# A linear-attention and SwiGLU block on one core: Q and K weights loaded together in 2 KB rows, token tiles loaded in pairs, and a new order of phase 1

## The chip, the cores and the metric

The kernel runs on one core of a Trainium2 chip. The metric is the device time of one execution in microseconds (us). A profiled execution gives the trace. In the profile PE is TensorE's matmuls and PEld its weight loads, DVE is VectorE, ACT is ScalarE, POOL is GpSimd, SP is SyncE, which here only issues DMAs.

## What is computed

```python
x = A_x                                   # [1, 2048, 512], bf16
xn = layernorm(x)                         # over the 512 columns, eps 1e-5
q, k, v = split(xn @ wqkv)                # wqkv [512, 1536]; 32 heads of 16
phi = lambda t: where(t > 0, t + 1, exp(t)) + 1e-6
kv = phi(k)^T v, z = sum over tokens of phi(k)        # per head
o = (phi(q) kv) / (phi(q) . z + 1e-6)
A = o @ wo                                # wo [512, 512]
B = (silu(xn @ w_gate) * (xn @ w_up)) @ w_down        # 512 -> 1792 -> 512
out = x + A + B
```

## The kernel before

The 2048 tokens are 16 tiles of 128, one token a partition. **Phase 1** handles each tile: load it, find mean and variance (`S`: `bn_stats`, line 260, and `bn_aggr`, line 266, on VectorE), 1/std on ScalarE (`R`, lines 275 and 277), normalise (`L` on VectorE, line 332; `P` on GpSimd, lines 347 and 350), transpose to columns x tokens, project to Q and K (`Q`, `K`: four matmuls of 512 columns each, one for each chunk of 128 rows of the weights, line 428), apply phi (exponential `y`, `x` on ScalarE, lines 446 and 449; clamp `n`, `m` on GpSimd, line 456; sum `u`, `s` on VectorE, line 467), and add the tile's part of G = xn^T phi(k) (`G`, four matmuls, line 477). V is never formed: kv comes from G and the V weights later (line 592). **Phase 2** computes gate and up (line 534), the product with silu, then for each tile the attention output and the down projection in one PSUM bank (lines 664 and 668), adds x (line 674) and stores.

Most tiles are transposed by DMA (`D`, line 406, SyncE's queue). The first four go another way. Tiles 0, 1 and 2 are only centred, not scaled; 1/std goes into the exponential's scale. They are *turned*: TensorE multiplies the raw x tile with an identity (`turn_x`, line 381) and adds minus the mean with a second product with a diagonal matrix of the mean (`turn_mean`, line 389; the diagonal at line 375, on VectorE by `a` or on GpSimd by `O`), and ScalarE or VectorE copy the halves out (`e`, `h` on ScalarE, line 398; `g`, `f` on VectorE, line 400). Tile 3 is normalised and then transposed on TensorE (`X`, line 362), and copied out by ScalarE (`Y`, line 370). The scaled copies that G needs of tiles 0 to 2 are `J` (GpSimd, line 327) and `j` (VectorE, line 319); `r` makes their powers of std on ScalarE.

The order is written out by hand. `load` (line 185) issues DMAs in two lists, one on SyncE's queue and one on ScalarE's, at the start: `h` is half a tile of x, `x` a tile, `Qc` and `Kc` chunk c of the Q or K weights. Then one long text names the steps; each step is added to its engine's list in the order of the text, and an engine works through its list in that order. `Q0:23` means chunks 2 and 3 of the Q projection of tile 0; `l` loads a tile on SyncE's queue; `F` is matmuls of 256 columns on constants, which keep TensorE busy (line 250, also used for warming up); `T0` to `T7` load the big weights on SyncE's queue (first halves of gate and up, V, wo, second halves of gate and up, two halves of down); `U` is the gate and up work of phase 2 brought forward. Waits between engines are found by `_Program` from the tiles that steps read and write.

Of the kernel before, what the change touches and what calls it, by code (L numbers as in the profile page):

```python
# [17 lines left out]
NDC = D // P  # L18
# [92 lines left out]


def bass_parallel_sum__linear_attn_block__swiglu_ffn__prompt_kernel(nc, A_x, A_wqkv, A_wo, B_x, B_w_gate, B_w_up, B_w_down, out):
    xin = A_x[0]
    oview = out[0]
    K = _Program()
    bf, f32 = dt.bfloat16, dt.float32

    with contextlib.ExitStack() as es:
        E = es.enter_context  # L120

        def sb(name, shape, dtype):
# [12 lines left out]
        wqkv = sb("wqkv", [P, NDC, 3 * D], bf)  # L135
# [18 lines left out]
        out_sb = sb("out_sb", [P, 2, D], bf)  # L154
# [25 lines left out]
        def B(i):  # L180
            return ("bank", i)


        def load(eng, key, dst, src):
            K.add(eng, lambda e: e.dma_start(dst, src), w=[key], dma=True)

        def xload(eng, t):
            load(eng, ("x", t), x_sb[:, t, :], xin[t * P:(t + 1) * P, :])

        def wload(eng, i, h=0, n=1):  # L190
            cs = slice(h * NDC // n, (h + 1) * NDC // n)
# [20 lines left out]
        H = D // 2  # L212

        def xhalf(eng, t, h):
            load(eng, ("x", t, h), x_sb[:, t, h * H:(h + 1) * H], xin[t * P:(t + 1) * P, h * H:(h + 1) * H])

        def wchunk(eng, i, c):
            load(eng, ("wqk", i, c), wqkv[:, c, i * D:(i + 1) * D], A_wqkv[c * P:(c + 1) * P, i * D:(i + 1) * D])

        for eng, text in (("sp", "h00 K0 x1 x3 Q1 K2"),  # L220
                          ("act", "h01 x2 Q0 Q3 Q2 K3 K1")):
            for w in text.split():
                if w[0] == "h":
                    xhalf(eng, int(w[1:-1]), int(w[-1]))
                elif w[0] == "x":
                    xload(eng, int(w[1:]))
                else:
                    wchunk(eng, int(w[0] == "K"), int(w[1:]))

        for i, v in enumerate((1e-5, math.log1p(1e-6), math.log(1e-6))):  # L230
# [3 lines left out]
            out=ident[:, :], in_=ident[:, :], compare_op=ALU.not_equal, fill=1.0,  # L234
# [159 lines left out]
        def turn_out(t, h, eng):  # L394
            src = banks[TURN_BANK[t] + h][:, 0:H].rearrange("p (c s) -> p c s", c=NDC // 2)
            dst = xcT[:, h * NDC // 2:(h + 1) * NDC // 2, t * P:(t + 1) * P]
            if eng == "act":
                K.add("act", lambda e: e.activation(dst, src, ACT.Copy), r=[B(TURN_BANK[t] + h)], w=[("xcT", t, h)])
            else:
                K.add("dve", lambda e: e.tensor_copy(dst, src), r=[B(TURN_BANK[t] + h)], w=[("xcT", t, h)])  # L400

# [16 lines left out]
        def proj(i, t, cs):  # L418
            if (i, t) not in at:
                at[i, t] = LOWBANK[i, t] if (i, t) in LOWBANK else nextbank()  # L420
                begun[i, t] = 0
            b, col = at[i, t], i * D
            src = xcT if t in CENTRED else xnT
            fns = []
            for c in cs:
                first, last = begun[i, t] == 0, begun[i, t] == NDC - 1
                begun[i, t] += 1
                fns.append(lambda e, c=c, first=first, last=last: e.matmul(  # L428
                    banks[b][:, :], src[:, c, t * P:(t + 1) * P], wqkv[:, c, col:col + D], start=first, stop=last))
            keys = sorted({("xcT", t, c // 2) for c in cs}) if t in CENTRED else xkeys(t)  # L430
            K.add("pe", fns, r=keys + [("wqk", i, c) for c in cs], w=[B(b)])
# [8 lines left out]
        def phi_exp(i, t):  # L440
            b = at[i, t]
            buf, bkey = ef[:, efslot(b), :], ("ef", efslot(b))
            if i == 0 and t in later:
                buf, bkey = pq[:, t, :], ("pq", t)
            if t in CENTRED:
                K.add("act", lambda e: e.activation(buf, banks[b][:, :], ACT.Exp, bias=lstd[:, t:t + 1], scale=rstd[:, t:t + 1]),  # L446
                      r=[B(b), ("rs", t), ("lstd", t)], w=[bkey])
            else:
                K.add("act", lambda e: e.activation(buf, banks[b][:, :], ACT.Exp), r=[B(b)], w=[bkey])  # L449

        def phi_min(i, t):
# [51 lines left out]
        def stat(t):  # L503
# [7 lines left out]
            "S": stat, "R": rs, "L": lna_dve, "P": lna_pool, "N": nmr, "A": lna_act, "D": dmat,  # L511
            "M": neg_mean, "a": lambda t: mean_diag(t) if t in TURN_BANK else centre_half(t, 0), "b": lambda t: centre_half(t, 1),
            "I": centre_mv, "O": lambda t: mean_diag(t, "pool"), "C": centre_dve, "B": centre_act, "E": centre_pool, "r": powers, "j": xg_dve, "J": xg_pool,
# [3 lines left out]
            "h": lambda t: turn_out(t, 1, "act") if t in TURN_BANK else evac(t, 2 * t + 1, "act", 2, 4), "f": lambda t: turn_out(t, 1, "dve") if t in TURN_BANK else evac(t, 2 * t + 1, "dve", 2, 4),  # L517
            "W": lambda t: transp(t, 2), "v": lambda t: evac(t, 2, "act"), "w": lambda t: evac(t, 2, "dve"),
            "X": lambda t: transp(t, 3), "Y": lambda t: evac(t, 3, "act"), "Z": lambda t: evac(t, 3, "dve"),
            "l": lambda t: xload("sp", t), "K": lambda t, cs=range(NDC): proj(1, t, cs), "x": lambda t: phi_exp(1, t), "m": lambda t: phi_min(1, t), "s": lambda t: phi_sum(1, t),  # L520
            "Q": lambda t, cs=range(NDC): proj(0, t, cs), "y": lambda t: phi_exp(0, t), "z": phi_keep, "n": lambda t: phi_min(0, t), "u": lambda t: phi_sum(0, t), "G": gacc, "F": lambda t: keep_busy(t, 256),
        }

# [40 lines left out]
        def run(text):  # L564
# [5 lines left out]
                steps[k](t) if cs is None else steps[k](t, cs)  # L570

        run("""
            F1 l4 S0 c0 S2 a2 S1 O0 R0 d0 c2 r0 e0 d2 f2 l13 h0 Q0:0 K0:0 J0 e2 Q2:0 K2:0 R2 r2 a1 J2 c1 l5 d1
            Q2:3 T1 S3 R1 Q0:3 Q0:1 Q2:2 g1 Q0:2 r1 Q2:1 K2:3 R3 j1 S4 y0 K0:3 K0:2 h1 l9 S13 K2:1 P3 K0:1 y2 x0
            n0 u0 K2:2 X3 x2 l6 K1:01 n2 m0 Q1:023 u2 m2 s0 K1:2 s2 l15 S9 Y3 l7 K1:3 Q1:1 K3 R13 x1 R4 y1 R9
            P13 L4 l14 x3 Q3 m1 s1 n1 D13 S5 G2 P9 y3 m3 u1 s3 G0 G1 D4 K13 D9 Q13 x13 n3 R5 m13 P5 u3 S14 l10
            s13 y13 n13 G3 S7 S10 K4 x4 K9 m4 Q9 R7 l8 G13 u13 x9 R10 D5 l11 m9 y9 s4 L10 R14 Q4 S8 s9 y4 l12 K5
            P7 D10 D7 x5 G4 n9 P14 n4 Q5 u9 S12 G9 m5 K10 u4 y5 K7 R8 R12 s5 n5 P8 u5 x10 Q10 S6 D14 m10 T5 s10
            G5 L12 y10 S11 K14 x7 Q7 m7 n10 R6 s7 G10 x14 y7 R11 L0 u10 S15 G7 T3 Q14 L6 y14 D8 m14 s14 R15 L1
            K8 D12 P11 n7 D11 Q8 x8 u7 n14 L15 G14 u14 L2 y8 K12 m8 K11 D6 n8 D15 x12 x11 m12 s8 D1 T0 Q6 y6 u8  # L580
            D2 K6 s12 x6 m11 n6 D0 Q12 T4 s11 u6 Q11 K15 y11 y12 G12 x15 T7 T2 G11 m6 s6 n12 Q15 m15 y15 G8 s15
            n15 u12 G15 u15 n11 u11 U0 U1 G6 T6
        """)

        def gt_evac(c, eng):
# [87 lines left out]
        def oout(bank, t, lo, hi):  # L673
            K.add("dve", lambda e: e.tensor_tensor(  # L674
                out=out_sb[:, t % 2, lo:hi], in0=banks[bank][:, 0:hi - lo], in1=x_sb[:, t, lo:hi], op=ALU.add),
                r=[B(bank)] + xk(t), w=[("ob", t % 2, lo)])
            K.add("sp", lambda e: e.dma_start(oview[t * P:(t + 1) * P, lo:hi], out_sb[:, t % 2, lo:hi]),
                  r=[("ob", t % 2, lo)], w=[("out", t, lo)], dma=True)

        def otile(t):  # L680
# [86 lines left out]
```

## Time and profile before

| what | value |
|---|---|
| median of three runs | 213.46 us (213.42 to 213.75) |
| the profiled execution, device time | 213.43 us |
| its span in the trace | 212.1 us |
| PE busy | 208.8 us, 98% of the span |
| DVE, ACT, POOL busy | 125.5, 67.3 and 66.5 us |
| Q and K projections (line 428) | 128 matmuls |
| DMA packets | 28894, 16.44 MB |
| first matmul of tile 13, the first tile transposed by DMA | starts at 17.05 us |
| last matmul ends | 209.97 us |

Matmuls overlap in the trace: one of 512 columns is listed with 0.38 us, but the next starts 0.216 us later. So TensorE's progress is read from starts. A line of the timeline merges equal instructions in a row: its start, its length, how many. What stands in brackets is the idle time of the engine ahead of it and what ended it. Landing times of DMAs are the issue's start plus the time to landing.

### The profile page before, as it was taken

To read this page: it belongs to the slowest core of one execution; us is meant where nothing else is said; L and a number is where in the kernel's file an instruction comes from. 1 tells how busy PE (TensorE), PEld (TensorE's weight loads), DVE (VectorE), ACT (ScalarE), POOL (GpSimd) and SP (SyncE) were. 2 spreads that over 40 slices of the span, in tenths; PEclk is the share of its full clock that TensorE was granted. 3 is DMA by queue.
4 is the path that set the end of the run, shared out by engine and by line. 5 is a ranking of instruction groups with operands and counts; after the bars stand their busy time and mean duration, and the time that the engine had idled before them with its cause. 6 is when DMAs were issued, how large, how long until landed. Compare 5 with 4: busy or idle time off the path is not lost.

```text
span 212.1 us, 2753 instructions
## 1 busy us (share of the span) xinstructions
PE 208.8 (98%) x1014; PEld 97.0 (46%) x1014; DVE 125.5 (59%) x226; ACT 67.3 (32%) x145; POOL 66.5 (31%) x92
## 2 busy tenths in 40 slices
PE   8999999999999999999999999999999999999995
PEld 4444444444544444444444444444444444444455
DVE  4898979845995458454644673464457473535121
ACT  4993665544445333031221322130123031220000
POOL 4587856539970153202102021202202220000000
DMA  5954568599401201120101120111001112011001
GB/s 166 362 166 102 125 214 159 88 327 352 151 0 25 53 0 25 25 53 25 25 25 36 39 29 25 25 49 26 28 29 22 25 49 53 0 49 43 31 28 51
DMA packets 28894, 16.44 MB, mean 78 GB/s; under 512 B 18640, under 2 KB 28752, under 8 KB 28880
## 3 DMA queue, kind: packets, MB, share of 16 engines
q1 hardware_dynamic: 27872, 15.41, 27.2%
q10 hardware_dynamic: 1008, 0.85, 1.2%
q8 instruction: 8, 0.13, 0.3%
q14 instruction: 6, 0.05, 0.1%
HBM read 9.96 MB, written 2.10 MB: 57 GB/s over the span
## 4 chain that ended last, share of the span: by engine, by line
PE 95%; DMA 2%; POOL 1%; ACT 1%; issue 0%; DVE 0%; POOLq 0%
PE pb L534 46%; PE pb L668 23%; PE pb L428 11%; PE pb L664 7%; PE pb L477 5%; PE pb L250 2%; DMA xnT<-xn 2%; POOL ef L456 1%; ACT ef L446 1%; PE pb L389 1%; PE pb L381 1%; PE pb L592 0%; PE pb L658 0%; POOL xn L350 0%; DVE out_sb L674 0%
## 5 line engine op out<-in xcount | busy, mean ns | idle before, releaser
L542 ACT ACTIVATE sil<-pb 128x512 bf16<-128x512 f32 x56 | 33.5, 597 | 102.9 <-PE pb L534 101.4
L547 DVE TENSOR_TENSOR hT<-pb,sil 128x512 bf16<-128x512 f32 x56 | 38.2, 683 | 37.1 <-PE pb L534 36.5
L534 PE MATMUL pb<-xnT,wg 128*128 128x512 bf16 x224 | 57.8, 379 | 0.0
L534 PE MATMUL pb<-xnT,wu 128*128 128x512 bf16 x224 | 57.8, 379 | 0.0
L668 PE MATMUL pb<-wd,hT 128*128 128x512 bf16 (+2 forms) x252 | 51.4, 355 | 0.0
L625 POOL TENSOR_TENSOR pz<-pq,zbc 128x512 f32<-128x512 bf16 x16 | 22.3, 1394 | 90.4 <-DVE den L632 79.6
L668 PEld LDWEIGHTS pb<-wd,hT 128*128 128x128 bf16 x252 | 23.6, 98 | 24.9
L534 PEld LDWEIGHTS pb<-xnT,wu 128*128 128x128 bf16 x224 | 21.9, 98 | 26.0
L534 PEld LDWEIGHTS pb<-xnT,wg 128*128 128x128 bf16 x224 | 21.9, 98 | 25.8
L674 DVE TENSOR_TENSOR out_sb<-pb,x_sb 128x512 bf16<-128x512 f32 (+2 forms) x18 | 11.4, 632 | 35.8 <-PE pb L668 35.8
L428 PE MATMUL pb<-wqkv,xnT 128*128 128x512 bf16 x104 | 24.2, 379 | 0.3 <-ACT xnT L370 0.2
L449 ACT ACTIVATE ef<-pb 128x512 bf16<-128x512 f32 x26 | 15.0, 593 | 14.0 <-PE pb L428 14.0
L456 POOL TENSOR_SCALAR ef<-ef 128x512 bf16<-128x512 bf16 x26 | 15.8, 615 | 10.9 <-ACT ef L449 10.8
L664 PE MATMUL pb<-M,pk 128*128 128x512 bf16 (+2 forms) x72 | 16.8, 355 | 0.0
L428 PEld LDWEIGHTS pb<-wqkv,xnT 128*128 128x128 bf16 x104 | 9.9, 98 | 13.2 <-ACT xnT L370 0.7
L477 PE MATMUL pb<-pk,xn 128*128 128x512 bf16 x52 | 12.9, 379 | 0.0
L647 DVE TENSOR_TENSOR pq<-pq,rden 128x512 bf16<-128x512 bf16 x16 | 12.6, 786 | 0.0
L467 DVE SCALAR_TENSOR_TENSOR pk<-pb,ef 128x512 bf16<-128x512 f32 x13 | 8.9, 684 | 4.1 <-POOL ef L456 4.1
L260 DVE BATCH_NORM_STATS2 stats<-x_sb 128x6 f32<-128x512 bf16 x15 | 10.2, 682 | 1.1 <-DMA x_sb<-in_A_x_dram 1.1
L632 DVE TENSOR_REDUCE den<-pz 128x32 f32<-128x512 f32 x16 | 10.8, 676 | 0.0
L500 POOL TENSOR_TENSOR zacc<-zacc,pk 128x512 f32<-128x512 f32 x8 | 10.6, 1322 | 0.6
L664 PEld LDWEIGHTS pb<-M,pk 128*128 128x128 bf16 x72 | 6.8, 98 | 7.4
(68 smaller groups left out, 115.4 us busy)
## 6 DMA issues: line engine op xcount, KB each, us to landing
out_dram<-out_sb SPq DMA_DIRECT2D x15, 128.0 KB, 1.7
x_sb<-in_A_x_dram SPq DMA_DIRECT2D x14, 128.0 KB, 5.3
wu<-in_B_w_up_dram SPq DMA_DIRECT2D x2, 896.0 KB, 6.2
wg<-in_B_w_gate_dram SPq DMA_DIRECT2D x2, 896.0 KB, 5.6
wd<-in_B_w_down_dram SPq DMA_DIRECT2D x2, 896.0 KB, 10.2
wqkv<-in_A_wqkv_dram ACTq DMA_DIRECT2D x5, 128.0 KB, 5.1
wo<-in_A_wo_dram SPq DMA_DIRECT2D x1, 512.0 KB, 6.5
wqkv<-in_A_wqkv_dram SPq DMA_DIRECT2D x1, 512.0 KB, 10.0
```

The source lines that it names most:

```text
L428: fns.append(lambda e, c=c, first=first, last=last: e.matmul(banks[b][:, :], src[:, c, t * P:(t + 1) * P], wqkv[:, c, col:col + D], start= ...
L449: K.add("act", lambda e: e.activation(buf, banks[b][:, :], ACT.Exp), r=[B(b)], w=[bkey])
L456: K.add("pool", lambda e: e.tensor_scalar(out=buf, in0=buf, scalar1=top, scalar2=0.0, op0=ALU.min, op1=ALU.max), r=[bkey] + tkeys, w=[bkey])
L477: K.add("pe", [(lambda e, c=c: e.matmul(banks[c][:, :], src[:, t, c * P:(c + 1) * P], pk[:, t, :], start=first, stop=last)) for c in range ...
L534: fns.append(lambda e, c=c, b=b, w_=w_: e.matmul(banks[b][:, :], w_[:, c, fc * P:(fc + 1) * P], xnT[:, c, C * 512:(C + 1) * 512], start=(c ...
L542: K.add("act", lambda e: e.activation(sil[:, j % 2, :], banks[gb(j)][:, :], ACT.Silu), r=[B(gb(j))], w=[("sil", j % 2)])
L547: K.add("dve", lambda e: e.tensor_tensor(out=hT[:, C % 2, fc, :], in0=banks[gb(j) + 1][:, :], in1=sil[:, j % 2, :], op=ALU.mult), r=[B(gb( ...
L625: K.add("pool", lambda e: e.tensor_tensor(out=pz[:, t % 2, :].rearrange("q (g p) -> q g p", g=NG), in0=pq[:, t, :].rearrange("q (g p) -> q ...
L647: K.add("dve", lambda e: e.tensor_tensor(out=heads(pq[:, t, :]), in0=heads(pq[:, t, :]), in1=rden[:, i, :][:, :, None].broadcast_to([P, NH ...
L664: fns = [(lambda e, g=g: e.matmul(banks[bank][:, 0:hi - lo], pk[:, t, g * P:(g + 1) * P], M[:, g, lo:hi], start=(g == 0), stop=False)) for ...
L668: fns = [(lambda e, fc=fc: e.matmul(banks[bank][:, 0:hi - lo], hT[:, C % 2, fc, jj * P:(jj + 1) * P], wd[:, fc, lo:hi], start=False, stop= ...
L674: K.add("dve", lambda e: e.tensor_tensor(out=out_sb[:, t % 2, lo:hi], in0=banks[bank][:, 0:hi - lo], in1=x_sb[:, t, lo:hi], op=ALU.add), r ...
```

## The change

- Token tiles: tile 2b + a now holds rows 256b + 2p + a (partition p), for loads and stores alike. So two tiles that belong together lie in rows of 2 KB in the device memory, and one load (`p` or `V`) brings both, 256 KB; a single tile (`x`, `h`) takes every other row.
- Weights: chunks 1, 2 and 3 of Q and K are each one load of 256 KB in rows of 2 KB (`W`); chunk 0 stays two loads. Steps that need either half wait for the whole.
- The start lists become `h00 K0 x1 W3 W2` on SyncE's queue and `h01 x2 Q0 W1 x3` on ScalarE's. The later tiles come in six pairs, issued on SyncE's queue right behind, ahead of the first half of the up weights and of all DMA transposes; before, some single tiles were issued between the transposes.
- Tile 1 is no longer turned. ScalarE finds its negated mean (`M`, line 289), VectorE centres it (`C`, line 304), TensorE transposes it (`W` in the text, line 362), VectorE copies it out (`w`, line 372).
- The text of phase 1 is a new order: two more fillers, one ahead of tile 0's projections and one ahead of tile 2's K; tile 2's diagonal by GpSimd; the statistics of tile 3 (`S3`) ahead of the copy `w1`; V and wo (`T2`, `T3`) ahead of the transposes of the last tiles; the second half of the gate weights (`T4`) last.

```diff
-TURN_BANK = {0: 0, 1: 2, 2: 2}
+TURN_BANK = {0: 0, 2: 2}
...
-    xin = A_x[0]
-    oview = out[0]
+    xin = A_x[0].rearrange("(b p a) d -> b p a d", p=P, a=2)
+    oview = out[0].rearrange("(b p a) d -> b p a d", p=P, a=2)
...
-            load(eng, ("x", t), x_sb[:, t, :], xin[t * P:(t + 1) * P, :])
+            load(eng, ("x", t), x_sb[:, t, :], xin[t // 2, :, t % 2, :])
...
+        def xpair(eng, t):
+            load(eng, [("x", t), ("x", t + 1)], x_sb[:, t:t + 2, :].rearrange("p a d -> p (a d)"),
+                 xin[t // 2].rearrange("p a d -> p (a d)"))
+
+        def qkchunk(eng, c):
+            load(eng, [("wqk", 0, c), ("wqk", 1, c)], wqkv[:, c, 0:2 * D], A_wqkv[c * P:(c + 1) * P, 0:2 * D])
+
-        for eng, text in (("sp", "h00 K0 x1 x3 Q1 K2"),
-                          ("act", "h01 x2 Q0 Q3 Q2 K3 K1")):
+        for eng, text in (("sp", "h00 K0 x1 W3 W2"),
+                          ("act", "h01 x2 Q0 W1 x3")):
...
-            F1 l4 S0 c0 S2 a2 S1 O0 R0 d0 c2 r0 e0 d2 f2 l13 h0 Q0:0 K0:0 J0 e2 Q2:0 K2:0 R2 r2 a1 J2 c1 l5 d1
-            Q2:3 T1 S3 R1 Q0:3 Q0:1 Q2:2 g1 Q0:2 r1 Q2:1 K2:3 R3 j1 S4 y0 K0:3 K0:2 h1 l9 S13 K2:1 P3 K0:1 y2 x0
-            n0 u0 K2:2 X3 x2 l6 K1:01 n2 m0 Q1:023 u2 m2 s0 K1:2 s2 l15 S9 Y3 l7 K1:3 Q1:1 K3 R13 x1 R4 y1 R9
+            S0 R0 S2 r0 O0 S1 F1 c0 d0 V12 e0 f0 c2 O2 d2 V4 M1 F1 C1 e2 R2 f2 Q0:0 J0 K0:0 Q2:0 K0:3 r2 Q2:1 W1
+            Q2:3 Q2:2 R1 Q0:3 K0:1 S3 r1 Q0:1 J2 Q0:2 w1 y2 R3 S13 y0 J1 L3 S4 K1:03 K0:2 n2 x0 F1 K2 n0 X3 m0
+            K1:2 R13 x2 K1:1 m2 V6 Q1:3 Q1:01 Q1:2 V8 V14 u0 s0 u2 s2 V10 Y3 T1 P13 R4 D13 Q3:03 S9 K3 x1 y1
...
-            K.add("sp", lambda e: e.dma_start(oview[t * P:(t + 1) * P, lo:hi], out_sb[:, t % 2, lo:hi]),
-            K.add("sp", lambda e: e.dma_start(oview[t * P:(t + 1) * P, lo:hi], out_sb[:, t % 2, lo:hi]),
+            K.add("sp", lambda e: e.dma_start(oview[t // 2, :, t % 2, lo:hi], out_sb[:, t % 2, lo:hi]),
```

More of the change, by code (lines that the diff above doesn't have):

```diff
@@ L184, in load @@
         def load(eng, key, dst, src):
-            K.add(eng, lambda e: e.dma_start(dst, src), w=[key], dma=True)
+            K.add(eng, lambda e: e.dma_start(dst, src), w=key if isinstance(key, list) else [key], dma=True)
         def xload(eng, t):
-            load(eng, ("x", t), x_sb[:, t, :], xin[t * P:(t + 1) * P, :])
+            load(eng, ("x", t), x_sb[:, t, :], xin[t // 2, :, t % 2, :])
         def wload(eng, i, h=0, n=1):
@@ L214, in xhalf @@
         def xhalf(eng, t, h):
-            load(eng, ("x", t, h), x_sb[:, t, h * H:(h + 1) * H], xin[t * P:(t + 1) * P, h * H:(h + 1) * H])
+            load(eng, ("x", t, h), x_sb[:, t, h * H:(h + 1) * H], xin[t // 2, :, t % 2, h * H:(h + 1) * H])
         def wchunk(eng, i, c):
             load(eng, ("wqk", i, c), wqkv[:, c, i * D:(i + 1) * D], A_wqkv[c * P:(c + 1) * P, i * D:(i + 1) * D])
-        for eng, text in (("sp", "h00 K0 x1 x3 Q1 K2"),
-                          ("act", "h01 x2 Q0 Q3 Q2 K3 K1")):
+        def xpair(eng, t):
[5 more added lines that the diff above has]
+                          ("act", "h01 x2 Q0 W1 x3")):
             for w in text.split():
@@ L226, in bass_parallel_sum__linear_attn_block__swiglu_ffn__prompt_kernel @@
                     xload(eng, int(w[1:]))
+                elif w[0] == "p":
+                    xpair(eng, int(w[1:]))
+                elif w[0] == "W":
+                    qkchunk(eng, int(w[1:]))
                 else:
@@ L519, in bass_parallel_sum__linear_attn_block__swiglu_ffn__prompt_kernel @@
             "X": lambda t: transp(t, 3), "Y": lambda t: evac(t, 3, "act"), "Z": lambda t: evac(t, 3, "dve"),
-            "l": lambda t: xload("sp", t), "K": lambda t, cs=range(NDC): proj(1, t, cs), "x": lambda t: phi_exp(1, t), "m": lambda t: phi_min(1, t), "s": lambda t: phi_sum(1, t),
+            "l": lambda t: xload("sp", t), "V": lambda t: xpair("sp", t), "K": lambda t, cs=range(NDC): proj(1, t, cs), "x": lambda t: phi_exp(1, t), "m": lambda t: phi_min(1, t), "s": lambda t: phi_sum(1, t),
             "Q": lambda t, cs=range(NDC): proj(0, t, cs), "y": lambda t: phi_exp(0, t), "z": phi_keep, "n": lambda t: phi_min(0, t), "u": lambda t: phi_sum(0, t), "G": gacc, "F": lambda t: keep_busy(t, 256),
@@ L572, in bass_parallel_sum__linear_attn_block__swiglu_ffn__prompt_kernel @@
         run("""
-            F1 l4 S0 c0 S2 a2 S1 O0 R0 d0 c2 r0 e0 d2 f2 l13 h0 Q0:0 K0:0 J0 e2 Q2:0 K2:0 R2 r2 a1 J2 c1 l5 d1
-            Q2:3 T1 S3 R1 Q0:3 Q0:1 Q2:2 g1 Q0:2 r1 Q2:1 K2:3 R3 j1 S4 y0 K0:3 K0:2 h1 l9 S13 K2:1 P3 K0:1 y2 x0
-            n0 u0 K2:2 X3 x2 l6 K1:01 n2 m0 Q1:023 u2 m2 s0 K1:2 s2 l15 S9 Y3 l7 K1:3 Q1:1 K3 R13 x1 R4 y1 R9
[L576 to L582, printed above, removed]
+            S0 R0 S2 r0 O0 S1 F1 c0 d0 V12 e0 f0 c2 O2 d2 V4 M1 F1 C1 e2 R2 f2 Q0:0 J0 K0:0 Q2:0 K0:3 r2 Q2:1 W1
+            Q2:3 Q2:2 R1 Q0:3 K0:1 S3 r1 Q0:1 J2 Q0:2 w1 y2 R3 S13 y0 J1 L3 S4 K1:03 K0:2 n2 x0 F1 K2 n0 X3 m0
+            K1:2 R13 x2 K1:1 m2 V6 Q1:3 Q1:01 Q1:2 V8 V14 u0 s0 u2 s2 V10 Y3 T1 P13 R4 D13 Q3:03 S9 K3 x1 y1
+            Q3:12 G0 m1 P4 s1 x3 y3 D4 n1 R9 L9 n3 u1 G2 G1 m3 K13 P1 x13 Q13 D9 u3 K4 m13 s3 S5 S10 R5 P5 s13
+            x4 m4 S7 R10 Q4 G3 D5 G13 K9 y13 y4 s4 n13 u13 R7 n4 L10 x9 S12 m9 G4 K5 x5 R12 P7 Q9 s9 m5 P12 u4
+            y9 S6 s5 S14 R6 G9 n9 D10 L6 u9 K10 Q5 x10 m10 y5 Q10 n5 y10 s10 D7 u5 n10 G5 S8 R14 D12 u10 K7 P14
+            Q7 S15 D6 x7 Q6 y7 m7 K6 s7 D14 T2 y6 x6 L0 n7 n6 G10 K12 m6 R15 u7 x12 u6 Q14 s6 P15 S11 T3 D15 R8
+            K14 Q12 R11 m12 L8 s12 D8 L11 G6 x14 y14 G7 Q15 y12 n14 u14 D11 y15 m14 G12 K8 D1 s14 n12 u12 T0 Q8
+            n15 u15 P2 x8 D0 y8 m8 s8 Q11 K11 K15 G14 n8 x11 y11 m11 u8 G8 D2 x15 T5 m15 s11 T6 s15 G11 n11 U0
+            G15 u11 U1 T7 T4
         """)
```

## The prediction

> **What bounds the kernel now.** I read first the busy time by stretches of the span, then TensorE's timeline at the ends of its idle time, then VectorE's timeline and the DMA issues beside it. The profiled execution took 213.43 us, of which 212.1 us are the span; the median of the runs is 213.46 us, so the sum is made against 213.43 and needs no correction. The busy time by stretches (columns: length, then busy us and instructions of PE, PEld, DVE, ACT, POOL, the clock, DMA share, GB/s):
>
> ```profile
> 5.00:10.00 5.00, 5.00 (x29) 2.42 (x26) 4.01 (x12) 4.57 (x23) 2.94 (x6) 1.00 1.02 355
> 10.00:15.00 5.00, 4.82 (x26) 2.19 (x25) 4.88 (x10) 4.91 (x13) 4.37 (x8) 1.00 0.58 195
> 15.00:17.05 2.05, 1.94 (x10) 0.69 (x8) 1.72 (x5) 0.95 (x2) 1.95 (x5) 1.00 0.64 131
> 17.05:62.00 44.95, 44.95 (x220) 20.78 (x221) 36.58 (x63) 23.47 (x52) 32.33 (x46) 1.00 0.66 176
> 62.00:210.00 148.00, 147.95 (x722) 68.95 (x719) 76.14 (x136) 31.43 (x54) 22.73 (x17) 1.00 0.13 31
> ```
>
> From 17.05 us to 210 us TensorE never stops: 192.90 of 192.95 us. The change leaves that work as it is, so the time is decided by **when TensorE reaches the matmul that now starts at 17.05 us**, K of tile 13. The timeline of TensorE ahead of it (start, length, engine, line, tile, idle before):
>
> ```profile
> 7.56 2.75 PE L428 MATMUL pb<-wqkv,hT 128*128 128x512 bf16 x12
> 10.15 0.39 PE L362 MATMUL pb<-ident,xn 128*128 128x128 bf16 x4
> ...
> 12.44 1.90 PE L428 MATMUL pb<-wqkv,xnT 128*128 128x512 bf16 x8 [0.18 <-ACT xnT L370]
> 14.18 2.75 PE L477 MATMUL pb<-pk,hT 128*128 128x512 bf16 x12
> 17.05 0.60 PE L428 MATMUL pb<-wqkv,xnT 128*128 128x512 bf16 x2
> ```
>
> Twelve matmuls start in 10.15 - 7.56 = 2.59 us, so one of 512 columns costs 0.216 us. By that step the eight of tile 3 could start at 12.09 (10.37 + 8 x 0.216) and start at 12.44: 0.35 us lost to the evacuation of tile 3's transposes. The twelve of G end at 14.18 + 2.59 = 16.77 and K of tile 13 starts at 17.05: 0.28 us lost to its DMA transpose. These 0.63 us, with some 0.03 us at the second turn's mean (5.31), are **all that a better order can win**. The rest of the first 5.7 us are warm-up matmuls and two turned tiles at 0.43 us for 512 columns, the same in both kernels.
>
> What threatens is the loading. VectorE's timeline and the DMA issues (KB each, us from issue to landing) of the issues at 2.19 and 2.22 us, and of those at 3.62 and 3.68 us:
>
> ```profile
> 6.85 0.69 DVE L260 BATCH_NORM_STATS2 stats<-x_sb 128x6 f32<-128x512 bf16 x1 [0.31 <-DMA x_sb<-in_A_x_dram]
> 7.58 0.18 DVE L266 BATCH_NORM_AGGREGATE mv<-stats 128x2 f32<-128x6 f32 x1
> 7.68 0.40 DVE L400 CAST hT<-pb 128x256 bf16<-128x256 f32 x1
> ```
> ```profile
> x_sb<-in_A_x_dram SPq DMA_DIRECT2D x1, 128.0 KB, 4.6
> wqkv<-in_A_wqkv_dram ACTq DMA_DIRECT2D x1, 128.0 KB, 4.8
> ```
> ```profile
> x_sb<-in_A_x_dram SPq DMA_DIRECT2D x1, 128.0 KB, 5.3
> wqkv<-in_A_wqkv_dram ACTq DMA_DIRECT2D x1, 128.0 KB, 5.5
> ```
>
> x3 lands at 2.19 + 4.6 = 6.8 us, and VectorE idles for it, ahead of the evacuation that tile 1 needs (line 400). The loads of place 7 of each queue land at 8.9 and 9.2 us. So **a load's place in the queue sets its landing**.
>
> **The change, part by part.** *TensorE's columns.* Tile 1's turn (4 x 128 and 2 x 256 columns, 7.12 to 7.56 = 0.44 us) becomes a transpose (10.15 to 10.37 = 0.22 us); two fillers of 256 columns come in, one at the half rate (0.22 us, the step 4.42 to 4.64 by the timeline of its stretch), one at the full rate (0.11 us). That is 0.22 won and 0.33 added: 0.1 us more. Tile 2's mean diagonal moves from VectorE (0.27) to GpSimd (0.37 in tile 0's row): TensorE waits for it, 0.1 us more.
>
> *ScalarE's queue.* Seven loads become five; its first statistics start when the issues are over, at 4.24 us, and may start 0.3 us earlier. The tile that waits for them stands behind TensorE's own order (second turn and filler until 6.0 us): nothing won. It gets the negated mean of tile 1, not in the trace: between 0.58 and 0.78 us, the 128x512 activations; I take 0.6. It lies between two evacuations, and the second needs the second turn anyway, done at about 5.75: nothing.
>
> *VectorE.* Tile 1's centring (0.38 to 0.41 us, the normalising rows) lies in its idle time before x3, where before had 0.31 us idle and two 0.4 us steps of tile 1's turn that go: nothing. But the evacuation of tile 1's transpose is new, 512 columns: between 0.40 us (half as many) and 0.69 (VectorE's copy of 512 f32 columns, line 589); I take 0.66. It stands **behind the statistics of x3**.
>
> *The loads.* Until x3 has landed, ScalarE's queue must bring 704 KB (64 + 128 + 128 + 256 + 128). The queues advance together; if they alternate row by row, SyncE's has then brought 832 KB, for its rows are of 2 KB. That is 1536 KB in all. Before, the pairs at 1408 and 1664 KB landed at 8.55 and 9.18 us (K3 and K1, issues at 3.19 and 3.68 with 5.4 and 5.5 us), so 1536 KB stand for about 8.87. Longer rows give some back. From 6 to 8 us, with rows of 1 KB, the queues moved 357 GB/s; from 8 to 10 us, mostly with rows of 1792 B, 381 GB/s: 7%. Of the 1536 KB, 896 are in 2 KB rows, 2.5 us at the former rate: 0.2 us, to 0.3 if the gain grows with the row. So x3 lands at about **8.5 to 8.6 us instead of 6.8**. W3 and W2 by their places (576 and 832 KB; before, 576 KB stood for 7.6 and 7.8) come at about 7.4 and 8.5; TensorE wants them at 6.95 and 7.9, waits of 0.45 and 0.2 us that hide in the next.
>
> *The new wait.* From x3's landing: 0.04 to start, 0.68 statistics, 0.04, 0.18 aggregate, 0.66 evacuation (0.08 overlapped), 0.05 to TensorE: 1.57 us. K of tile 1 can't start before 8.5 + 1.57 = 10.07 us. Without any wait TensorE would be there at 5.71 + 0.1 + 0.22 (Q0 starts) + 0.9 (three matmuls while the clock comes up, as 5.71 to 6.57 to 6.90 show) + 8 x 0.216 + 0.22 = 8.9 us. Behind the waiting matmul stand tile 2's K, tile 3's transpose and all of G; nothing else feeds TensorE.
>
> *From there.* 13 matmuls, one transpose and one filler: 2.81 + 0.22 + 0.11 = 3.13, so 13.2 us; tile 3's evacuation then stands behind four exponentials of 0.68 us steps and ends at about 13.3: 0.15 us wait instead of 0.35, since TensorE is late itself. Then 8 + 12 matmuls, 4.31 us: **K of tile 13 at 17.65 us, against 17.05: +0.6 us**.
>
> *Later.* The paired x loads put 512 KB more into SyncE's queue ahead of the first DMA transpose: (512 KB at 0.36 KB/ns, 1.4 us, less 0.35 for longer rows) the queue runs dry at about 15.0 instead of 13.96 us. Tile 13's transpose is issued at about 14.4 and lands 2.45 us (the common case) to 3.23 us (13.77 to 17.00, behind running loads) later: 16.9 to 17.6, just covered. If TensorE were early, this would take up to 0.3 us. V and wo, 1 MB, now go out ahead of tile 15's transpose: before, wu and wo ahead of a transpose landed 5.2 and 6.5 us after issue; I find tile 15's landing within 0.6 us of its use, either side, and take 0 with +0.5 as the bound. The single x loads that go from between the transposes free SyncE, which waits for data there: nothing. The other gate half goes out last of the big ones, at about 60 us by four such loads of 2.4 to 4 us each, wanted at 62.6. Every store writes every other row, pieces as long as before: 1.6 us from issue to landing at the end, +-0.1.
>
> Sum: 213.43 + 0.6 = **214.0 us**.
>
> **A rule against it.** The Trainium skill, DMA: Bandwidth & Descriptors, Specifications, puts the least transfer for line rate at 512 B, so rows of 2 KB would bring nothing. The 7% between rows of 1 KB and of 1792 B speak against it; by the rule x3 lands at 8.87, and the time is 0.3 us above the forecast.
>
> **The rivals.**
> - *Forecast* (0.42): 213.7 to 214.4, x3 at 8.2 to 8.9 us.
> - *x3 in time* (0.36), the other side. Some of the 16 DMA engines lag: until 6.8 us the queues had moved about 1.4 MB (0.02, 0.51 and 0.57 in stretches of 2 us, then 0.8 us at 357 GB/s), though x3 and Q3 close only the first 0.9 MB. If this lag doesn't come again, x3 lands up to 0.9 us earlier, at 7.6; the wait shrinks to 0.3 us, most of which tile 3's wait takes back. Below 7.3 us nothing waits on x3, K of tile 13 can start at 16.8, and only its transpose holds it. Price: -0.25 to +0.3, 213.2 to 213.7. It decides from x3 at 7.7 us: there +0.0.
> - *Both old waits vanish* (0.05): -0.6, 212.8. Against it: tile 3's evacuation still stands behind four exponentials.
> - *SyncE's queue becomes the bound* (0.11): the transposes of tile 13 or 15 land late on top of the forecast, 214.5 to 215.
> - *Rows of 2 KB bring nothing* (0.06): +0.9, 214.3.
>
> **The numbers.** About 0.2% (0.43 us) is what a measurement can tell from no change. Faster by more than that: the third rival, and some mass for an order that I misjudge, 0.11. Slower: most of the forecast, the last two: 0.51. Within: 0.38. Eight in ten lie between 213.1 and 214.8: the second rival's best case below, the transposes' bound above. The forecast alone: 213.7 to 214.4.
>
> **What would show it.** In the changed kernel's profile VectorE should wait for x3 until about 8.5 us, and TensorE should idle before K of tile 1, released by VectorE's copy of the transpose; K of tile 13 should start at 17.6. Wrong if x3's statistics start before 8 us, if TensorE idles elsewhere after 18 us, or if K of tile 13 starts before 17.1.

## The result, and the profile after

The changed kernel takes **214.84 us** (median of 18 executions, 213.59 to 216.36) against 213.44 us (18 of before, 212.96 to 213.88): a ratio of 1.0067, 95% interval 1.0047 to 1.0087. It is slower, as forecast, but by 1.4 us instead of 0.6, just above the range of 213.1 to 214.8. And it scatters: over 2.8 us, where before stays within 0.9 us here (in the session of e1 to e4, 33 of 35 executions of before lay between 212.9 and 214.2 us, and two took 215.5).

The profiled execution took 214.88 us (span 213.2). All lines of the kernel lie 11 lower in the listing now (428 is 439). First TensorE's timeline of the changed kernel ahead of K of tile 13 (start, length, engine, line, tile, idle before):

```profile
6.30 0.39 PE L400 MATMUL pb<-dgm,const-bfloat16-1.0 128*128 128x256 bf16 x2 [1.01 <-POOL dgm L386]
6.53 0.27 PE L261 MATMUL pb<-const-bfloat16-1.0 128*128 128x256 bf16 x1
6.64 0.81 PE L439 MATMUL pb<-wqkv,hT 128*128 128x512 bf16 x3
8.15 0.61 PE L439 MATMUL pb<-wqkv,hT 128*128 128x512 bf16 x2 [0.70 <-DMA wqkv<-in_A_wqkv_dram]
...
10.61 0.82 PE L439 MATMUL pb<-wqkv,hT 128*128 128x512 bf16 x3 [0.19 <-DVE hT L383]
...
13.88 1.90 PE L439 MATMUL pb<-wqkv,xnT 128*128 128x512 bf16 x8
15.61 2.75 PE L488 MATMUL pb<-pk,hT 128*128 128x512 bf16 x12
18.61 0.60 PE L439 MATMUL pb<-wqkv,xnT 128*128 128x512 bf16 x2 [0.24 <-DMA xnT<-xn]
```

K of tile 13 starts at 18.61 us instead of 17.05: 1.56 us late, where 0.6 had been forecast. Read by starts (a matmul of 512 columns every 0.216 us), TensorE waits here for W3 (6.64 + 3 x 0.216 = 7.29 to 8.15: 0.86 us), for tile 1's copy ahead of 10.61 (8.81 + 6 x 0.216 = 10.11, so 0.5 us), for tile 3's evacuation (0.1 us) and for tile 13's DMA transpose (15.61 + 12 x 0.216 = 18.20 to 18.61: 0.4 us). Behind that the two kernels run alike: the first attention matmul of phase 2 starts at 86.85 us against 85.38, still 1.47 us apart.

The busy time of the changed kernel by stretches (length, then busy us and instructions of PE, PEld, DVE, ACT, POOL, clock, DMA share, GB/s) shows the loss in the first alone: TensorE is busy for 3.29 of 5 us, where it was for all 5.00.

```profile
5.00:10.00 5.00, 3.29 (x21) 1.52 (x20) 3.34 (x8) 3.84 (x19) 3.19 (x7) 1.00 1.00 344
10.00:15.00 5.00, 4.76 (x25) 2.04 (x25) 4.89 (x12) 4.91 (x13) 3.53 (x6) 1.00 0.89 328
```

VectorE's timeline of the changed kernel, and its DMA issues at 2.19 us (W3) and 2.70 us (x3), with KB and us to landing:

```profile
9.34 0.69 DVE L271 BATCH_NORM_STATS2 stats<-x_sb 128x6 f32<-128x512 bf16 x1 [1.59 <-DMA x_sb<-in_A_x_dram]
10.06 0.18 DVE L277 BATCH_NORM_AGGREGATE mv<-stats 128x2 f32<-128x6 f32 x1
10.16 0.39 DVE L383 COPY hT<-pb 128x512 bf16<-128x512 bf16 x1
```
```profile
wqkv<-in_A_wqkv_dram SPq DMA_DIRECT2D x1, 256.0 KB, 5.9
```
```profile
x_sb<-in_A_x_dram ACTq DMA_DIRECT2D x1, 128.0 KB, 6.6
```

The forecast wait is there, with its releaser: VectorE idles for x3, which lands at 9.31 us, and the copy that TensorE needs stands behind it. But W3 also lands late, at 8.1 us, and that wait comes first.

The profile can also follow the work back from a late instruction, at each step to what released it. Some steps of this chain ahead of K of tile 13 in the changed kernel (start, length, what):

```profile
2.19 5.91 DMA wqkv<-in_A_wqkv_dram
8.15 0.61 PE pb L439 x2
...
9.60 0.78 ACT ef L457
...
12.67 0.68 ACT ef L457
13.43 0.69 POOL ef L467
...
14.38 0.77 POOL xn L361
15.17 3.39 DMA xnT<-xn
18.61 3.63 PE pb L439 x16
```

The chain goes from W3's landing to TensorE's next projections, through the exponentials on ScalarE (`ef`, line 457) and GpSimd's clamp and normalising of tile 13 to that tile's DMA transpose. Tile 1's copy does not stand in it. x3 is close to it all the same: its statistics end at 10.24 us (10.06 + 0.18), and ScalarE, which then needs them for tile 3's 1/std, is done with its first exponential at 10.37. The transpose was issued at 15.17 us, where before issued it at 13.77: 1.40 of the 1.56 us.

### The profile page after: what moved, and what is told of

It is laid out like the page before. It is cut to its first block, busy times and chain, and to the rows that moved or that the text cites. A ratio compares the mean times of both kernels' runs of the same rounds, so it can differ in the third digit from the quotient of the medians.

```text
span 213.2 us, 2724 instructions
## 1 busy us (share of the span) xinstructions
PE 207.1 (97%) x995; PEld 96.2 (45%) x1014; DVE 123.8 (58%) x224; ACT 68.1 (32%) x145; POOL 68.5 (32%) x97
## 4 chain that ended last, share of the span: by engine, by line
PE 91%; DMA 4%; ACT 2%; POOL 1%; issue 1%; SPq 1%; DVE 0%
PE pb L545 45%; PE pb L679 23%; PE pb L439 10%; PE pb L675 6%; PE pb L488 5%; DMA wqkv<-in_A_wqkv_dram 3%; DMA xnT<-xn 2%; ACT ef L457 1%; SPq L185 1%; PE pb L603 0%; PE pb L669 0%; POOL xn L361 0%; POOL ef L467 0%; ACT rstd L288 0%; ACT lnv L286 0%
## 5 line engine op out<-in xcount | busy, mean ns | idle before, releaser
L545 PE MATMUL pb<-xnT,wg 128*128 128x512 bf16 x215 | 55.9, 379 | 0.0
L439 PE MATMUL pb<-wqkv,xnT 128*128 128x512 bf16 x101 | 23.6, 379 | 0.3 <-DMA xnT<-xn 0.2
L478 DVE SCALAR_TENSOR_TENSOR pq<-pb,ef 128x512 bf16<-128x512 f32 x13 | 8.8, 684 | 2.8 <-POOL ef L467 2.8
```

What stands on the lines that cost most here:

```text
L439: fns.append(lambda e, c=c, first=first, last=last: e.matmul(banks[b][:, :], src[:, c, t * P:(t + 1) * P], wqkv[:, c, col:col + D], start= ...
L478: K.add("dve", lambda e: e.scalar_tensor_tensor(out=dst, in0=val, scalar=low, in1=mid, op0=ALU.max, op1=ALU.add), r=keys + lkeys, w=[dkey])
L545: fns.append(lambda e, c=c, b=b, w_=w_: e.matmul(banks[b][:, :], w_[:, c, fc * P:(fc + 1) * P], xnT[:, c, C * 512:(C + 1) * 512], start=(c ...
```

## The experiments

Three theories stand against each other, told here by their content, since the letters in the expectations are each text's own. **The copy**, the recorded one: tile 1's copy behind x3's statistics delays TensorE. **The loads**: the new loads of the Q and K weights land too late for TensorE, whatever the order. **The order**: the new order or tile 1's new way costs. Times are medians; the ratio, with its interval, is to before in the same session, and is not exactly that of the medians.

| run | us (range) | ratio (95% interval) |
|---|---|---|
| changed | 214.84 (213.59 to 216.36) | 1.0067 (1.0047 to 1.0087) |
| e1 rows of the tiles alone | 213.35 (212.77 to 214.07) | 0.9992 (0.9966 to 1.0019) |
| e2 start lists and weight loads alone | 214.69 (213.73 to 215.23) | 1.0048 (1.0019 to 1.0076) |
| e3 order and tile 1 alone | 214.15 (213.89 to 215.77) | 1.0036 (1.0007 to 1.0066) |
| e4 both, tiles in the old rows | 214.53 (214.03 to 216.69) | 1.0055 (1.0025 to 1.0086) |
| e5 copy ahead of x3's statistics | 214.64 (214.45 to 214.77) | 1.0062 (1.0047 to 1.0076) |
| e6 up weights later | 215.37 (214.02 to 215.86) | 1.0085 (1.0059 to 1.0110) |
| e7 each weight load as two | 213.62 (213.22 to 214.42) | 1.0016 (1.0003 to 1.0029) |
| e8 half the weight bytes | 213.27 (212.77 to 213.77) | 1.0004 (0.9992 to 1.0015) |
| e9 weight loads of 256 KB in 1 KB pieces | 214.62 (213.78 to 216.49) | 1.0062 (1.0033 to 1.0091) |
| e10 as e7, waits for both halves | 214.03 (213.71 to 215.08) | 1.0036 (1.0022 to 1.0050) |
| e13 as e10, halves by partitions, 2 KB rows | 214.86 (214.67 to 215.14) | 1.0079 (1.0065 to 1.0094) |
| e14 as e13, 1 KB pieces | 215.32 (214.87 to 215.90) | 1.0092 (1.0078 to 1.0106) |

### One part alone (e1 to e4)

```diff
 e1: before, and
+    xin = A_x[0].rearrange("(b p a) d -> b p a d", p=P, a=2)   # and oview; loads and stores follow
 e2: before, and
+        for eng, text in (("sp", "h00 K0 x1 W3 W2"), ("act", "h01 x2 Q0 W1 x3")):
 e3: changed, with before's lists, tiles of 128 rows in a row, pairs as two loads
+        for eng, text in (("sp", "h00 K0 x1 x3 Q1 K2"), ("act", "h01 x2 Q0 Q3 Q2 K3 K1")):
 e4: changed, with tiles of 128 rows in a row (pairs still one load)
```

> The kernel before with one part of the change alone: tile 2b + a holds every other row of 256 tokens, for loads and stores. Place theory (the loss comes from x3's and W3's later places in the queues, and from what is queued behind x3's statistics): no load changes its place, so 0.0, within 0.2 us of the kernel before. Row theory (reading 1 KB pieces at 2 KB pitch slows the first loads, x2 landed at 4.84 us instead of 4.01): +0.5 to +1.0 us, and x2 lands 0.5 us later than before.

> The kernel before with the new start lists alone (chunks 1 to 3 of Q and K as one load each in 2 KB rows, x3 last on ScalarE's queue); rows, order of phase 1 and single x loads as before. Place theory: x3 lands at about 8.5 us instead of 6.8, and the old text too has x3's statistics ahead of an evacuation of tile 1 on VectorE: +0.7 to +1.3 us. Row theory: x3 is read in one piece, 0.0 to +0.3 us.

> The new order of phase 1 with tile 1 centred by VectorE, but the old start lists, contiguous rows, and pairs as two loads of 128 KB. Place theory: x3 lands at 6.8 us, nothing waits behind it, -0.2 to +0.1 us. Row theory: 0.0 too. If the order itself is the loss, +0.7 us or more.

> The changed kernel with contiguous tiles (a pair is one load of two runs of 1 KB rows); lists and order as changed. Place theory: all of the loss stays, +1.2 to +1.6 us against the kernel before. Row theory: half or more of it goes, +0.2 to +0.7 us.

The rows of the tiles and of the stores cost nothing that shows (e1). The lists alone cost most of the loss (e2, 0.48%), with before's own order and before's turned tile 1. In e2's profile (213.88 us, one of its short executions) the chain goes through x3, which the lists put last: it landed at 8.54 us instead of 6.83. With the tiles in their old rows the loss stays (e4, 0.55%), as expected if the rows are free.

The order alone costs too (e3, 0.36%), where the expectation had nothing unless the order itself is the loss. But its one long wait is a mismatch: it wants K3 first, and the old lists bring K3 at 8.26 us. So e3 doesn't show that the order costs by itself. TensorE's timeline of e3:

```profile
8.30 0.60 PE L439 MATMUL pb<-wqkv,hT 128*128 128x512 bf16 x2 [1.41 <-DMA wqkv<-in_A_wqkv_dram]
```

### The copy ahead of x3's statistics (e5)

```diff
-  K0:1 S3 r1 Q0:1 J2 Q0:2 w1 y2
+  K0:1 r1 Q0:1 J2 Q0:2 w1 S3 y2
```

> The changed kernel, but the copy of tile 1's transpose (w1) stands ahead of the statistics of x3 (S3) on VectorE. The wait of 0.5 us before K of tile 1 in the changed kernel's profile then goes. Theory of the prediction (that wait is the price): -0.4 to -0.5 us against the changed kernel. Rival (the price is the landing of the weights: four exponentials stand behind Q of tile 2, and tile 3's copy and tile 13's transpose behind those, whoever waits first): the wait moves to tile 3's copy, -0.1 to 0.1 us.

If the copy were the price, this would give most of it back. It gives 0.2 us, within the scatter. TensorE's timeline of e5 tells why:

```profile
7.99 0.62 PE L439 MATMUL pb<-wqkv,hT 128*128 128x512 bf16 x2 [0.90 <-DMA wqkv<-in_A_wqkv_dram]
...
8.67 2.28 PE L439 MATMUL pb<-wqkv,hT 128*128 128x512 bf16 x9
...
18.39 0.82 PE L439 MATMUL pb<-wqkv,xnT 128*128 128x512 bf16 x3 [0.22 <-DMA xnT<-xn]
```

K of tile 1 now runs straight on (nine matmuls in a row from 8.67 us), but TensorE had already waited for W3 until 7.99, and what it wins it loses again at tile 3's evacuation (at 13.68 us) and at tile 13's transpose. The chain is that of the changed kernel: W3 (landed 7.95), exponentials, GpSimd, the transpose issued at 14.97. The copy is a wait that exists, not the price.

### The up weights later (e6)

```diff
-  Y3 T1 P13 R4 D13 ...  Q13 D9 u3
+  Y3 P13 R4 D13 ...  Q13 D9 T1 u3
```

> The changed kernel, but the first half of the up weights (896 KB) is issued on SyncE's queue behind the first three DMA transposes instead of ahead of them. In the changed kernel's profile tile 13's transpose was issued at 15.17 us while that load still ran (landed 15.53) and took 3.39 us instead of 2.45. If the running load is what delays it: it lands 2.5 us after issue, the wait of 0.4 us before K of tile 13 goes, -0.3 to -0.4 us against the changed kernel. If not: 0.0.

The running load is not what delays it. The load of the up weights left the stretch ahead of tile 13's transpose; the transpose still took 3.38 us (15.31 to 18.69), and the kernel got no faster.

The landing records of the transpose point elsewhere. It is done in 16 parts; in the changed kernel fifteen of them had landed 2.54 us after the issue, and the last one came 0.85 us later. At 17.03 us, in the middle of it, runs a packet of 8 KB on another queue (q14), which the profile lists as `instruction`. The first transpose of before has both too: last part 0.73 us behind, such a packet at 15.61 us. All profiles are counted in the last section.

### The same bytes as two loads, and fewer bytes (e7, e8)

```diff
 e7
-        for eng, text in (("sp", "h00 K0 x1 W3 W2"), ("act", "h01 x2 Q0 W1 x3")):
+        for eng, text in (("sp", "h00 K0 x1 K3 Q3 Q2 K2"), ("act", "h01 x2 Q0 Q1 K1 x3")):
 e8: W loads the Q half alone; K of chunks 1 to 3 reads Q's weights
-            load(..., wqkv[:, c, 0:2 * D], A_wqkv[c * P:(c + 1) * P, 0:2 * D])
+            load(..., wqkv[:, c, 0:D], A_wqkv[c * P:(c + 1) * P, 0:D])
```

> The changed kernel, but each W load is two loads of 128 KB in rows of 1 KB, in the same places (SyncE's queue: h00 K0 x1 K3 Q3 Q2 K2; ScalarE's: h01 x2 Q0 Q1 K1 x3). Place theory (bytes ahead in the queue decide): the half that is wanted first lands 0.3 to 0.5 us earlier, x3 0.2 us later, -0.3 to +0.2 us against the changed kernel. If the long rows themselves are slow (long packets of 0.8 to 1.3 us among them): -0.8 us or more.

> The changed kernel, but the K halves of chunks 1 to 3 are left out: each W load brings the Q half alone (128 KB), and K's matmuls of these chunks read Q's weights. Order and number of instructions are as changed; 384 KB less are ahead of x3. If the loads are the loss: W3 and x3 land 1 us or more earlier, and the time falls by 1.2 to 1.8 us, to the kernel before or below it. If the new order or tile 1's new path is the loss: it stays within 0.4 us of the changed kernel.

e8 computes K with the weights of Q in three of four chunks. With half the bytes the loss is gone (ratio 1.0004), with the changed order and tile 1's new way in place: W3's place is filled at 6.78 us and x3 lands at 7.72. The order theory falls, except for lists that do not fit it (e3); the loads theory stands. And e7, with all the bytes at the same places, wins 1.2 of the 1.4 us back by splitting three loads. That is the size that its expectation gave to slow long rows; the next runs test them. TensorE's timeline of e7:

```profile
6.04 0.59 PE L439 MATMUL pb<-wqkv,hT 128*128 128x512 bf16 x2 [0.16 <-DMA wqkv<-in_A_wqkv_dram]
7.08 0.81 PE L439 MATMUL pb<-wqkv,hT 128*128 128x512 bf16 x3 [0.45 <-DVE hT L411]
...
11.42 0.40 PE L373 MATMUL pb<-ident,xn 128*128 128x128 bf16 x4 [0.38 <-DVE xn L343]
...
17.45 1.89 PE L439 MATMUL pb<-wqkv,xnT 128*128 128x512 bf16 x8
```

No wait for chunks 1 to 3 is left (the one at 6.04 is for chunk 0 of Q, landed 5.90); two waits for VectorE are. The second goes back to a load as well: VectorE waits until 9.76 us for the pair of tiles 12 and 13, and its statistics stand ahead of tile 3's normalising. Among the runs that compute the right result it is the fastest form of the changed order, and it is not faster than before.

### What it is about a larger load (e9, e10, e13, e14)

The rows (2 KB against 1 KB), the size (256 KB against 128), and the one landing for both halves change together between the changed kernel and e7. These runs take them apart (SBUF is the on-chip memory; its 128 partitions hold the 128 rows of a chunk):

```diff
 e9: SBUF order Q, V, K: the same loads of 256 KB, cut into 1 KB pieces
+COL = {0: 0, 1: 1024, 2: 512}
-            load(..., wqkv[:, c, 0:2 * D], A_wqkv[c * P:(c + 1) * P, 0:2 * D])
+            load(..., wqkv[:, c, :].rearrange("p (i f) -> p i f", i=3)[:, 0::2, :],
+                 A_wqkv[c * P:(c + 1) * P, 0:2 * D].rearrange("p (i f) -> p i f", i=2))
 e10: e7, and
-            K.add("pe", fns, r=keys + [("wqk", i, c) for c in cs], w=[B(b)])
+            K.add("pe", fns, r=keys + [("wqk", j, c) for c in cs for j in ((0, 1) if c else (i,))], w=[B(b)])
 e13: e10, and for chunks 1 to 3, i = 0 and 1:
+                lo = i * P // 2
+                load(eng, ("wqk", i, c), wqkv[lo:lo + P // 2, c, 0:2 * D], A_wqkv[c * P + lo:c * P + lo + P // 2, 0:2 * D])
 e14: e13, with e9's SBUF order and its 1 KB pieces
```

> The changed kernel with the V columns put between those of Q and K in SBUF: each load of a chunk of Q and K is still one DMA of 256 KB at the same place of the same queue, but it is cut into pieces of 1 KB, since its two halves no longer lie side by side. Theory A (the length of the rows: pieces of 2 KB make some of the 16 engines lag, and a load lands when the last one is done): W3 lands at about 7 us and x3 at about 8.0 us, as with split loads, K of tile 13 starts at 17.5 to 17.8, 213.6 to 213.9 us. Theory B (the size of the load: 256 KB have one landing, and what waits for half of it waits for all): W3 at about 8, x3 at 9.2, K of tile 13 at about 18.5, 214.6 to 214.9 us, as in the changed kernel. Prediction's own terms: 2 KB rows win 0.2 to 0.3 us, so that this kernel would be slower than the changed one, 215.0.

> The kernel of the run with split loads (128 KB each, 213.62 us), with one thing changed: every matmul of Q and K of the chunks 1 to 3 waits for both halves of its chunk, as it must when the chunk comes as one load. The loads, their places and the order of the work are the same. Theory B (one landing for 256 KB makes TensorE wait for bytes that it doesn't yet need): most of the microsecond between split and whole loads comes back, 214.2 to 214.7 us, K of tile 13 at 18.0 to 18.5. Theory C (a load of 256 KB itself lands later than the same bytes as two loads: in the profiles Q3 landed at 6.86 and x3 at 7.95 with split loads, W3 at 7.53 to 8.10 and x3 at 8.77 to 9.31 with whole ones, bar the run of the lists alone with 7.25 and 8.54): coarse waits cost only what lies between K3 and Q3, 6.41 to 6.86, most of which stands beside the wait for the evacuation at 7.08: 213.6 to 213.8 us, K of tile 13 at 17.4 to 17.7.

> As the run of split loads with coarse waits (128 KB loads, 1 KB rows, every matmul of chunks 1 to 3 waits for both halves, 214.03 us), but each chunk is split into its upper and lower 64 partitions instead of its Q and K columns: the same number of loads of the same 128 KB at the same places, in rows of 2 KB. Theory A (the rows: packets of 2 KB stall for longer, in six of seven profiles with 2 KB weight rows two to five packets took over 1 us, in the seven with 1 KB rows none or one): 214.5 to 214.9 us, with packets over 1 us in the profile. Theory B (the size of the load, whatever its rows): 213.9 to 214.2 us, as with 1 KB rows, and few or no such packets. Prediction's own term (2 KB rows give 0.2 to 0.3 us back): 213.7 to 213.9 us.

> As the run of half loads by partitions (64 partitions each, 128 KB, waits for both halves, 214.86 us), but with the V columns between those of Q and K in SBUF, so that every load is cut into pieces of 1 KB instead of rows of 2 KB. Theory A (the rows): back to the 214.0 us of the split by columns, 213.8 to 214.3, and no or one packet over 1 us between 3 and 9 us. Theory F (loads of 64 partitions are slower, whatever their rows): 214.6 to 215.0 us, as with 2 KB rows.

**The rows are not it.** Two pairs differ in little else: 256 KB loads, 1.0067 with 2 KB rows and 1.0062 with 1 KB; half loads of 64 partitions, 1.0079 and 1.0092. In neither pair are the longer rows slower by more than the intervals allow, and the second leans to the longer rows. By itself e13, 0.8 us above e10, fits theory A; e14 shows that those 0.8 us belong to loads of 64 partitions. The issue of one takes 0.55 to 0.87 us in the trace, against 0.41 to 0.45 for the loads of 128 partitions in e10, and the last weight load lands at 9.42 and 9.46 us instead of 8.92.

**The one landing costs a part.** Waits for both halves, with nothing else changed, take 0.4 us (e10 against e7). That is little above the noise, since the two intervals overlap by a little, and it lies between the two expectations. TensorE's timeline of e10, whose wait ends with Q3 at 7.80 us, though the matmul needs K3 alone (7.06):

```profile
5.97 0.81 PE L439 MATMUL pb<-wqkv,hT 128*128 128x512 bf16 x3
7.85 0.60 PE L439 MATMUL pb<-wqkv,hT 128*128 128x512 bf16 x2 [1.07 <-DMA wqkv<-in_A_wqkv_dram]
```

The 0.6 to 0.8 us that remain between e10 and whole loads are not settled. Whole loads may themselves land later: in the eight profiles with them x3, with the same bytes ahead of it, landed at 8.54 to 10.01 us, in the two with the split by columns at 7.95 (e7) and 8.72 (e10). Two profiles do not show it.

### The changed kernel again (e11, e12)

The loads of e7 and e10 are the same, yet Q3 landed at 6.86 and 7.80 us. Two more profiles of the changed kernel, without any edit, tell how much of this is chance.

> The changed kernel once more, unchanged, for a second profile of it. Theory D (the landings of the first loads vary from execution to execution by about 1 us, and the changed kernel, whose TensorE waits on three of them, takes over what it gets: the two kernels with the same split loads had Q3 at 6.86 and 7.80, x3 at 7.95 and 8.72): W3 lands somewhere between 7.2 and 8.4, x3 between 8.5 and 9.5, not at the same times as in the first profile (8.10, 9.31), and the start of K of tile 13 moves with them, at 17.4 to 18.9. Theory E (the loads of 256 KB land late always, by the same amount): W3 at 8.0 to 8.2 and x3 at 9.2 to 9.4 again, K of tile 13 at 18.5 to 18.7, 214.7 to 215.0 us.

> The changed kernel a third time, for a third profile, with the same expectations: by theory D other landings again (W3 between 7.2 and 8.4, x3 between 8.5 and 9.5) and a K of tile 13 that follows them between 17.4 and 18.9; by theory E W3 at 8.0 to 8.2, x3 at 9.2 to 9.4, K of tile 13 at 18.5 to 18.7.

| | first | e11 | e12 |
|---|---|---|---|
| device time, us | 214.88 | 216.71 | 215.47 |
| W3 lands | 8.10 | 8.77 | 8.46 |
| x3 lands | 9.31 | 10.01 | 9.68 |
| K of tile 13 starts | 18.61 | 20.41 | 19.03 |

In kind theory D holds: the landings move by 0.7 us from execution to execution, and the end moves with them. Its ranges do not: all six values of e11 and e12 lie above them, so what this kernel gets is later than the theory had it. Each load has 16 landing records, one for each DMA engine that works on it. The times at which these finished their parts of W3, in order:

```
first  5.14 6.00 6.19 6.36 6.41 6.48 6.66 6.80 6.82 6.86 6.87 6.92 7.38 7.94 8.00 8.10
e11    5.11 5.52 6.03 6.03 6.09 6.23 6.27 6.28 6.29 6.33 6.36 6.36 6.37 6.38 8.62 8.77
e12    5.05 5.33 5.47 5.84 6.12 6.13 6.18 6.19 6.22 6.25 6.26 6.27 6.28 6.41 6.55 8.46
```

In e12, 15 of 16 parts had landed by 6.55 us; the last one came 1.9 us later. Among the packets of these microseconds one of 2048 B took 2.00 us, from 4.87; such a packet usually takes 0.084 us. In e11 three took 1.24 to 1.44 us. The Trainium skill, DMA: Bandwidth & Descriptors, "Why a DMA increments its semaphore by 16 and not by 1", says that the engines of a DMA finish independently and only the full count means that all has landed; the three rows above show it, and what it costs.

TensorE's timeline of e11, then its busy time by stretches (columns as above):

```profile
6.10 0.81 PE L439 MATMUL pb<-wqkv,hT 128*128 128x512 bf16 x3
8.81 0.78 PE L439 MATMUL pb<-wqkv,hT 128*128 128x512 bf16 x2 [1.90 <-DMA wqkv<-in_A_wqkv_dram]
...
9.81 3.45 PE L439 MATMUL pb<-wqkv,hT 128*128 128x512 bf16 x9
```
```profile
7.00:9.00 2.00, 0.19 (x1) 0.10 (x1) 0.21 (x1) 1.39 (x9) 1.69 (x3) 1.00 1.04 391
9.00:11.00 2.00, 2.00 (x9) 1.01 (x9) 0.93 (x3) 0.09 (x1) 0.00 (x0) 0.53 1.05 404
```

After 1.9 us without work the granted clock fell to about half until 12.5 us, and nine matmuls took 3.45 us that took 2.28 in e5: 1.2 us more. The mean clock of e11 is 0.992; of the 18 timed executions of the changed kernel the longest (216.36 us) shows that too, and the other 17 show 1.000. In e12 the wait was 1.86 us and the clock stayed at 1.00. This is a second cost of a late load, and it came in few executions.

## Why the prediction was right in direction and wrong in size

- **The step that failed: when the loads land, and which of them decides.** "W3 and W2 come at about 7.4 and 8.5": 8.10 and 9.12 us (8.77 and 9.82, 8.46 and 9.49 in the other profiles). "x3 lands at about 8.5 to 8.6": 9.31, 10.01, 9.68. The step took a load's place in the queue for its landing, read from one profile of before; the runs show that the slowest of 16 engines sets it, and that this moves by 0.7 us between three executions of one kernel. The prediction had seen that some engines lag, but let the lag of before only shrink (*x3 in time*); here it came again, and larger.
- **"Waits of 0.45 and 0.2 us that hide in the next"**: the path was wrong too. Read by starts, the wait for W3 was 0.86 us (2.06 and 2.08 in e11 and e12). It hides in the wait for the copy only on TensorE's own timeline. The chain to K of tile 13 runs from W3 through the exponentials and GpSimd to tile 13's transpose, and with the copy out of the way (e5) nearly all of the loss stays. x3's statistics came only 0.13 us ahead of that chain, so by this profile x3 would have cost nearly as much with W3 in time.
- **Tile 13's transpose "just covered"**: 0.4 us of wait. It was issued at 15.17 us, not at about 14.4, and took 3.39 us where 2.45 had been taken as the common case and 3.23 as the bound. These 0.77 and 0.16 us make up nearly all of the 0.96 us by which K of tile 13 missed its forecast. Counted along TensorE instead, 0.54 is K of tile 1 (10.61 against 10.07) and 0.42 this wait.
- **The direction**: the loads did come later and did cost, as forecast, but not through the copy, on which the 0.6 us were worked out. So the sign was not mere luck, but the size rested on a path that did not decide.
- **What bounds the kernel**: right. TensorE has no idle time of weight behind K of tile 13. Its start moved by 1.56 us, the profiled device time by 1.45.
- **Columns, centring, stores, rows of the tiles, the later order**: right, at nothing (e1; 86.85 against 85.38 far behind). Tile 2's diagonal on GpSimd and x2 (landed 4.84 instead of 4.01) put Q0 of tile 0 at 6.64 instead of 6.0; in e11 and e12 it was 6.10 and 5.77. It hid behind W3, as all ahead of it did.
- **The copy of tile 1**: 0.39 us, not 0.66. The chain from x3's landing to K of tile 1 was 10.61 - 9.31 = 1.30 us, not 1.57.
- **"2 KB rows give 0.2 to 0.3 us back"**: not seen. The sum counts 896 KB in such rows, but the three W loads are 768 KB and x3 comes in rows of 1 KB; by the same working that is 0.15 us. The two pairs of rows above agree with the rival that such rows bring nothing, and with the rule of the Trainium skill, DMA: Bandwidth & Descriptors, Specifications, on which that rival leaned. Longer rows do win later, where one queue loads alone (last section), but no win shows in the first 9 us.
- **The other rivals**: x3 came in time in no profile of the changed kernel. "SyncE's queue becomes the bound" named the right range (214.5 to 215) with half of the right mechanism: the transpose was late, but the load ahead of it was not the cause (e6). That the price lay in the weight loads themselves was in none.

## What to carry to other kernels

A load that an engine waits for lands with the slowest of its 16 parts, and at this kernel's start that part came up to about 2 us behind the others. Merging two loads there made TensorE wait for bytes that it did not need yet, and splitting them again won 1.2 of the 1.4 us: keep what is needed first as a load of its own, or have other work ready. Take a landing time from several profiles before an order is built on it. And follow the chain back from the matmul that decides: the wait that shows on the busiest engine need not be on it.

## What the runs showed of the hardware

- Single DMA packets of 1 to 2 KB took 0.6 to 2.0 us between 3 and 9 us of the span in every profile but one (e8), where 0.046 us (1 KB) and 0.084 us (2 KB) are usual. Packets over 1 us came 2 to 5 times in each profile of the changed kernel, and not at all in those of before, e9, e10 and e14; the pairs of rows show no time lost by that difference.
- The first DMA transpose took 3.2 to 3.5 us in thirteen of sixteen profiles, and 2.50 to 2.73 us in three; most of the later ones took about 2.45. In the thirteen, one of its 16 parts came 0.7 to 0.9 us behind the other fifteen, and an `instruction` packet of 8 KB ran 1.8 to 2.0 us after the issue. In the three it ran 1.2 us after the issue, or only when the transpose had landed. Five later transposes with such a packet 1.8 to 2.0 us after the issue had a last part 0.8 to 1.9 us late as well. One transpose in all had a part that late without such a packet at that time (e14). Both kernels have this delay at tile 13. That the packet is its cause fits all these cases, but no run removed it.
- Behind the start, pairs of x tiles in 2 KB rows on SyncE's queue alone landed every 0.68 us for 256 KB; as 1 KB pieces (e4), every 0.75 us. There the longer rows do help, though nothing waits for these pairs in the changed kernel (in e7 VectorE waits for the first).
- TensorE's clock fell to half after 1.90 us of idle time (e11), and not after 1.86 us (e12): about the same pause did it once and once not. The Trainium skill, TensorE: Matmul & The Clock Gate, Part 1, gives at least one idle window of about 3.4 us for it; here less was enough once.
